# Recurrence and soft mixture of experts: output stored in units of 16 rows per partition instead of 8, with the short last part stored early

## The chip, the cores and the metric

The kernel runs on one core of one Trainium2 chip. The metric is the device time in microseconds of one execution; lower is better. Before the change the median of four runs is 205.44 us (204.38 to 205.74). The profile is one further execution, taken by the hardware profiler.

## The reference

Four sequences of 5056 tokens with 256 channels go through a gated recurrence, and its output through a soft mixture of experts with 8 experts of 4 slots, so 32 slots. Cut to what matters:

```python
sig = 1.0 / (1.0 + np.exp(-f_logit))
f = lower_bound + (1.0 - lower_bound) * sig
for t in range(S):                       # S = 5056, 4 sequences
    h = f[:, t] * h + (1.0 - f[:, t]) * x[:, t]
    y[:, t] = h
x = y.reshape(4 * 5056, 256)

logits = x @ phi                         # 20224 x 32
d = softmax(logits, axis=0)              # over all tokens
slot_input = d.T @ x                     # 32 x 256
slot_out = relu(slot_input[e] @ w1[e]) @ w2[e]    # per expert, 4 slots each
c = softmax(logits, axis=1)              # over the 32 slots
out = c @ slot_out                       # 20224 x 256, float32
```

The output is 20.7 MB. None of it can be computed before `slot_out` is known, and `slot_out` needs the logits of all tokens.

## The kernel before, in words

The first stage reads 41.4 MB of `f_logit` and `x` in 40 units of 512 tokens of one sequence. ScalarE makes the gates (L188), GpSimd the products (L199), TensorE transposes both to channels (L214), VectorE runs the scan (L247), TensorE transposes the result back to tokens (L260) and makes logits (L288), and ScalarE writes their exponentials, without the division, into `etall` as bf16: the 32 slots of the four sequences stand on 128 partitions, the tokens along the free dimension (L297). The order of this stage is written out by hand in the loop over `n`. Of the ten groups of 512 tokens the last begins at 4544, so that it ends at 5056, and the group before it, `odd`, has 448 tokens.

The weights `w1` and `w2` (16.8 MB read) are loaded by GpSimd's queue, beside the first stage and after it. The middle stage (L505 to L603) runs the experts on the 32 slots and ends in `slot_out`, which L603 scales. Inside it the row sums of `etall` over the slots are made as matmuls with ones (`row_sums`, L321), some before the experts and the others after the first eighth of the last accumulation; `rrow` gets their reciprocals (L529, L602). The 64 tokens of each sequence that don't fill three rows of 128 partitions stand in `left`, which four GpSimd copies fill (`left_over`, L331).

The store stage (L606 to L684) computes and stores the output. A matmul (L622) has 128 tokens' weights from `etall` as its stationary operand, read with a step of `n_r` tokens, and `slot_out` as its moving operand, and gives 128 tokens by 256 channels in `op` (PSUM, four buffers of four such rows). VectorE (`by_vector`, L611, four rows in one instruction) or ScalarE (`by_scalar`, L616, one row in each) multiplies by the reciprocal row sum into `ob` (SBUF), and SyncE's queue stores `ob`. With `n_r` rows per partition, partition `p` holds tokens `p * n_r` to `p * n_r + n_r - 1` of its unit, so each partition's store is one run of `n_r` KB in memory.

Before, a unit is 1024 tokens of one sequence, `n_r` = 8, 1 MB; there are 16 (L659), of which the first goes out in six pieces (L656). After them come, for each sequence, 384 tokens with `n_r` = 3 (L667), the left-over 64 tokens of all sequences in two stores (L683), and the last 512 tokens with `n_r` = 4 (L667). `ob` has four buffers; a buffer is taken again when its store has landed.

Of the kernel before, what the change touches and what calls it, by code (L numbers as in the profile page):

```python
# [9 lines left out]
F32 = mybir.dt.float32  # L10
# [8 lines left out]
def kernel(  # L19
# [40 lines left out]
    def part_rows(g):  # L60
        return R3 if g == odd else R
# [45 lines left out]
    etall = store.tile([P, n_grp * G], BF16, name="etall")  # L107
    rrow = store.tile([P, n_grp, R, B], F32, name="rrow")
# [29 lines left out]
    with tc.tile_pool(name="sp2", bufs=3) as sp2, \  # L138
# [154 lines left out]
        def exps(g):  # L293
            gs = batch_of(g)
            if g == gs[-1]:
                T = sum(rows(i) for i in gs) * R
                nc.scalar.activation(etall[:, ds(gs[0] * G, T)], lgs[0][:, :T], ACT.Exp,  # L297
                                     accum_out=csum[:, ds(g, 1)])

        def weights_to_tokens(g):  # L300
            gs = batch_of(g)
            if g != gs[-1]:
                return
            ep = plg.tile([P, 2, R, P], BF16, name="ep", tag="lg")
            for i, k in enumerate(gs):
                n_p = rows(k)
                ew = etall[:, ds(k * G, n_p * R)].rearrange("s (p r) -> s p r", r=R)
                for r in range(R):
                    nc.tensor.transpose(ep[:n_p, i, r], ew[:, :, r], ident)
            et = etok.tile([P, 2, R, B, NS], BF16, name="et", tag="et")  # L310
            n_p, k = rows(g), len(gs)
            nc.vector.tensor_copy(et[:n_p, :k].rearrange("p g r b s -> p (g r b s)"),  # L312
                                  ep[:n_p, :k].rearrange("p g r s -> p (g r s)"))
            for i, k in enumerate(gs):
                ets[k] = et[:, i]

        def row_sums(g):
            n_r = part_rows(g) if g >= odd else 2 * R
            ew = etall[:, ds(g * G, P * n_r)].rearrange("s (p r) -> s p r", r=n_r)
            for r in range(n_r):  # L320
                nc.tensor.matmul(rs_ps[:, g + r // R, r % R], ew[:, :, r], ones,  # L321
                                 start=True, stop=True, skip_group_check=True)
            if g == odd:
                nc.tensor.matmul(rs_ps[:, g, R3, ds(0, B // 2)],
                                 left.rearrange("s t u -> s (t u)"), pair_ones,
                                 start=True, stop=True, skip_group_check=True)

        def left_over():
            for b in range(B):
                k = ds(b * NS, NS)  # L330
                nc.gpsimd.tensor_copy(left[k, :, b % 2], etall[k, ds(odd * G + P * R3, L)])  # L331
# [29 lines left out]
        def late_exps(bs):  # L361
            k = ds(bs[0] * NS, len(bs) * NS)
            nc.scalar.activation(etall[k, ds(last * G, G)], lgs[0][k, ds(G, G)], ACT.Exp,
                                 accum_out=csum[k, ds(last, 1)])

        def late_weights(bs, copy):
            k, w = ds(bs[0] * NS, len(bs) * NS), len(bs) * NS
            ew = etall[k, ds(last * G, G)].rearrange("s (p r) -> s p r", r=R)
# [7 lines left out]
        def odd_weights():  # L376
            n_p = rows(odd)
            ets[odd] = etok.tile([P, R, B, NS], BF16, name="et", tag="et")
            ew = etall[:, ds(odd * G, n_p * R)].rearrange("s (p r) -> s p r", r=R)
# [30 lines left out]
        for n in range(n_unit):  # L410
# [10 lines left out]
            else:  # L421
# [34 lines left out]
                if n == n_unit - 2:  # L456
                    tail = psp.tile([P, 2, G], F32, name="tail", tag="sp")
                    rs_ps = tail[:, 0, ds(0, n_grp * R * B)].rearrange(
                        "p (g r b) -> p g r b", r=R, b=B)
# [5 lines left out]
                    left_over()  # L465
# [5 lines left out]
            if n == n_unit - 1:  # L471
                logits(last, [0, 1, 2])
                late_exps([0, 1, 2])
                for g in range(0, 4, 2):
                    row_sums(g)
# [22 lines left out]
        late_exps([3])  # L498
        to_tokens(n_unit - 1)
# [16 lines left out]
    with tc.tile_pool(name="ew", bufs=1) as ew, \  # L516
# [12 lines left out]
        nc.vector.reciprocal(rrow[:, :4], rs_ps[:, :4])  # L529
# [56 lines left out]
        for j in range(Q):  # L586
# [5 lines left out]
            if j == 0:  # L592
                nc.tensor.matmul(so_ps, rep2, so4, start=False, stop=False,
                                 skip_group_check=True)
                for g in [*range(4, odd, 2), odd, last]:
                    row_sums(g)
                for part, ps in ((rrow[:, 4:odd], rs_ps[:, 4:odd]),
                                 (rrow[:, odd, ds(0, R3)], rs_ps[:, odd, ds(0, R3)]),
                                 (rrow[:, odd, R3, ds(0, B // 2)],
                                  rs_ps[:, odd, R3, ds(0, B // 2)]),  # L600
                                 (rrow[:, last], rs_ps[:, last])):
                    nc.vector.reciprocal(part, ps)  # L602
# [4 lines left out]
    with tc.tile_pool(name="pout", bufs=4, space=PSUM) as pout, \  # L607
         tc.tile_pool(name="osb", bufs=4) as osb:

        def by_vector(ob, op, r, k, scale):  # L610
            nc.vector.tensor_tensor(ob[:, ds(r, k)], op[:, ds(r, k)],  # L611
                                    scale.broadcast_to([P, k, D]), ALU.mult)

        def by_scalar(ob, op, r0, k, scale):
            for i in range(k):
                nc.scalar.activation(ob[:, r0 + i], op[:, r0 + i], ACT.Copy, scale=scale[:, i])  # L616

        def share(g, n_r, b, rs):
            op = pout.tile([P, R, D], F32, name="op", tag="op")
            ew = etall[:, ds(g * G, P * n_r)].rearrange("s (p r) -> s p r", r=n_r)  # L620
            for i, r in enumerate(rs):
                nc.tensor.matmul(op[:, i], ew[ds(b * NS, NS), :, r],  # L622
                                 slot_out[ds(b * NS, NS), :],
                                 start=True, stop=True, skip_group_check=True)
            return op

        def rows_of(g, n_r, b):
            return out[ds(b * S + first(g), P * n_r)].rearrange("(p r) d -> p r d", r=n_r)

        for g in range(0, odd, 2):  # L630
            scales = rrow[:, ds(g, 2)].rearrange("p g r b -> p (g r) b")
            for b in range(B):
                n_r = 2 * R
                dst = rows_of(g, n_r, b)
                head = g == 0 and b == 0
                scale = scales[:, :, ds(b, 1)]
                if not head:
                    ob = osb.tile([P, n_r, D], F32, name="ob", tag="ob")
                for h in range(2):
                    ops = [share(g, n_r, b, range(h * R, h * R + R))] if not head else [  # L640
                        share(g, n_r, b, range(r, r + R // 2))
                        for r in (h * R // 2, R + h * R // 2)]
                    if not head:
                        by = by_vector if h == 0 else by_scalar
                        by(ob[:, ds(h * R, R)], ops[0], 0, R, scale[:, ds(h * R, R)])
                        continue
                    if h == 0:
                        obs = [osb.tile([P, n_r, D], F32, name="ob", tag="ob")
                               for _ in range(2)]
                    k = 1 if h == 0 else 2  # L650
                    for i in range(0, R // 2, k):
                        for j, by in enumerate((by_vector, by_scalar)):
                            r = h * R // 2 + i
                            by(obs[j][:, ds(h * R // 2, R // 2)], ops[j], i, k,
                               scale[:, ds(j * R + r, k)])
                            nc.sync.dma_start(out=dst[:, ds(j * R + r, k)],  # L656
                                              in_=obs[j][:, ds(r, k)])
                if not head:
                    nc.sync.dma_start(out=dst, in_=ob)  # L659

        for g in (odd, last):
            n_r = part_rows(g)
            for b in range(B):
                ob = osb.tile([P, R, D], F32, name="ob", tag="ob")
                by = (by_vector, by_scalar)[b % 2]
                by(ob, share(g, n_r, b, range(n_r)), 0, n_r, rrow[:, g, ds(0, n_r), ds(b, 1)])
                nc.sync.dma_start(out=rows_of(g, n_r, b), in_=ob[:, :n_r])  # L667
            if g == odd:
                n_p = B // 2
                op = pout.tile([P, R, D], F32, name="op", tag="op")  # L670
                ob = osb.tile([P, R, D], F32, name="ob", tag="ob")
                for j in range(n_p):
                    k = ds(j * 2 * NS, 2 * NS)
                    nc.tensor.matmul(op[:, j * R // n_p], left[k].rearrange("s t u -> s (t u)"),
                                     slot_out[k, :], start=True, stop=True,
                                     skip_group_check=True)
                scale = rrow[:, odd, R3, ds(0, n_p)].unsqueeze(2)
                nc.vector.tensor_tensor(
                    ob[:, ds(0, n_p)], op.rearrange("p (j k) d -> p k j d", j=n_p)[:, 0],
                    scale.broadcast_to([P, n_p, D]), ALU.mult)  # L680
                for j in range(n_p):
                    dst = out.rearrange("(b t) d -> t b d", b=B)
                    nc.sync.dma_start(  # L683
                        out=dst[ds(first(odd) + P * R3, L), ds(2 * j, 2)], in_=ob[:, j])  # L684
# [30 lines left out]
```

## Time and profile before

| What | Value |
|---|---|
| median of 4 runs | 205.44 us (204.38 to 205.74) |
| the profiled execution: time, span | 204.62 us, 202.9 us |
| busy: PE, DVE, ACT, POOL | 134.8, 144.9, 139.2, 99.2 us |
| moved by DMA | 70.74 MB, mean 349 GB/s |
| HBM read, written | 58.23 MB, 20.71 MB |
| 1 MB stores (L659) | 15, median 8.1 us from issue to landing |
| 512 KB stores (L667, last group) | 4, median 3.2 us |
| first store issued, by SyncE's queue | 148.46 us |
| end of the last store packet | 201.3 us |

The busy times are totals over stages that have different limits; which of them bounds a stage is read from the waits of that stage. A DMA's rate counts the bytes that it writes: the weights arrive as float32 and are written as bf16, so their rate of about 210 GB/s is twice that in reads. PEclk in the profile is the clock granted to TensorE, in tenths; it is 5 in the store stage from 152 us on.

### The profile page before, as it was taken

To read this page: it belongs to the slowest core of one execution; us is meant where nothing else is said; L and a number is where in the kernel's file an instruction comes from. 1 tells how busy PE (TensorE), PEld (TensorE's weight loads), DVE (VectorE), ACT (ScalarE), POOL (GpSimd) and SP (SyncE) were. 2 spreads that over 40 slices of the span, in tenths; PEclk is the share of its full clock that TensorE was granted. 3 is DMA by queue.
4 is the path that set the end of the run, shared out by engine and by line. 5 is a ranking of instruction groups with operands and counts; after the bars stand their busy time and mean duration, and the time that the engine had idled before them with its cause. 6 is when DMAs were issued, how large, how long until landed. Compare 5 with 4: busy or idle time off the path is not lost.

```text
span 202.9 us, 3118 instructions
## 1 busy us (share of the span) xinstructions
PE 134.8 (66%) x1096; PEld 100.4 (49%) x1097; DVE 144.9 (71%) x164; ACT 139.2 (69%) x195; POOL 99.2 (49%) x70
## 2 busy tenths in 40 slices
PE   0585484973966767595876776989879577762320
PEld 0364363763756546574655565657765344431110
DVE  1699869797897999979999999724184445553160
ACT  3588665899986999879988596533077666663260
POOL 2488586894978459971996959930000000000000
PEclk9999979698896999969999999999995555555555
DMA  5999999999999999999999999999449999999986
GB/s 196 412 411 409 409 413 407 407 410 308 427 405 368 358 417 408 336 395 397 373 287 406 322 237 210 216 211 216 90 168 420 417 417 423 418 423 414 407 318 266
DMA packets 19054, 70.74 MB, mean 349 GB/s; under 512 B 2256, under 2 KB 3536, under 8 KB 17120
## 3 DMA queue, kind: packets, MB, share of 16 engines
q1 hardware_dynamic: 16560, 62.14, 76.7%
q0 software_dynamic: 2336, 8.42, 20.7%
q8 instruction: 8, 0.13, 0.3%
q14 instruction: 6, 0.05, 0.1%
q10 hardware_dynamic: 144, 0.00, 0.0%
HBM read 58.23 MB, written 20.71 MB: 389 GB/s over the span
## 4 chain that ended last, share of the span: by engine, by line
DMA 44%; DVE 22%; PE 13%; ACT 8%; issue 7%; POOL 3%; SPq 0%; ACTq 0%; DVEq 0%; POOLq 0%
DMA out_dram<-ob 17%; DVE h L247 15%; DMA f_t<-in_f_logit_dram 11%; DMA w_sb<-in_moe_w_dram 9%; DMA x_t<-in_x_dram 8%; PE hp L260 3%; PE sp L214 3%; DVE ht L274 3%; DVE ob L611 3%; ACT s_t L188 2%; ACT ob L616 2%; PE up L214 2%; PE op L622 2%; ACT a L237 2%; POOL w_sb L122 2%
## 5 line engine op out<-in xcount | busy, mean ns | idle before, releaser
L199 POOL TENSOR_TENSOR u_t<-s_t,x_t 128x1024 bf16<-128x1024 bf16 (+1 forms) x39 | 82.5, 2127 | 29.4 <-ACT s_t L188 22.1
L247 DVE TENSOR_TENSOR_SCAN h<-a,h,up 128x512 bf16<-128x512 f32 (+1 forms) x72 | 86.2, 1250 | 5.3 <-PE up L214 3.7
L260 PE MATMUL hp<-ident_f,h 128*128 128x128 f32 (+1 forms) x160 | 31.6, 324 | 31.4 <-DVE ht L274 19.4
L616 ACT ACTIVATE ob<-op,rrow 128x256 f32<-128x256 f32 x78 | 30.3, 480 | 27.0 <-DMA out_dram<-ob 17.8
L188 ACT ACTIVATE s_t<-f_t 128x2048 bf16<-128x2048 f32 (+2 forms) x23 | 38.5, 1673 | 12.9 <-DMA f_t<-in_f_logit_dram 12.8
L237 ACT ACTIVATE a<-sp,nomlb 128x1024 f32<-128x1024 bf16 (+2 forms) x46 | 43.3, 992 | 5.2 <-PE sp L214 4.3
L260 PEld LDWEIGHTS hp<-ident_f,h 128*128 128x128 f32 (+1 forms) x160 | 23.2, 208 | 41.9 <-DVE ht L274 24.0
L622 PE MATMUL op<-slot_out,etall 32*128 32x256 bf16 x156 | 31.1, 382 | 15.1 <-DVE ob L611 10.2
L611 DVE TENSOR_TENSOR ob<-op,rrow 128x1024 f32<-128x1024 f32 (+3 forms) x22 | 23.9, 1101 | 22.4 <-DMA out_dram<-ob 18.2
L622 PEld LDWEIGHTS <-etall 32*128 32x128 bf16 x156 | 18.9, 147 | 26.9 <-issue 22.4
L214 PE MATMUL sp<-ident_f,s_t 128*128 128x128 f32 x144 | 23.5, 312 | 9.2 <-ACT s_t L188 5.9
L214 PE MATMUL up<-ident_f,u_t 128*128 128x128 f32 x144 | 25.3, 304 | 0.8 <-POOL u_t L199 0.8
L214 PEld LDWEIGHTS sp<-ident_f,s_t 128*128 128x128 f32 x144 | 19.6, 164 | 10.5 <-issue 5.9
L214 PEld LDWEIGHTS up<-ident_f,u_t 128*128 128x128 f32 x144 | 19.6, 160 | 1.9 <-POOL u_t L199 1.2
L274 DVE COPY ht<-hp 128x512 f32<-128x512 f32 (+1 forms) x22 | 14.7, 670 | 3.1 <-PE hp L260 3.1
L274 ACT COPY ht<-hp 128x512 f32<-128x512 f32 (+1 forms) x18 | 10.4, 580 | 5.3 <-PE hp L260 5.3
L247 DVE TENSOR_TENSOR_SCAN h<-a,up 128x512 bf16<-128x512 f32 x8 | 9.4, 1210 | 0.8 <-PE up L214 0.7
L288 PE MATMUL lg<-h,phi 128*32 128x512 bf16 (+1 forms) x80 | 7.3, 413 | 0.0
L338 PE MATMUL slot_ps<-ht,et 128*32 128x256 bf16 (+1 forms) x144 | 6.0, 289 | 0.8 <-DVE et L312 0.8
L188 ACT ACT_TABLE_LOAD x4 | 5.1, 1283 | 1.2 <-PEq L699 1.2
L297 ACT ACT_TABLE_LOAD x4 | 5.1, 1283 | 0.1
L338 PEld LDWEIGHTS <-et 128*32 128x32 bf16 (+1 forms) x144 | 3.5, 99 | 2.7 <-DVE et L312 0.9
(88 smaller groups left out, 89.1 us busy)
## 6 DMA issues: line engine op xcount, KB each, us to landing
f_t<-in_f_logit_dram SPq DMA_DIRECT2D x36, 512.0 KB, 10.7
x_t<-in_x_dram SPq DMA_DIRECT2D x36, 512.0 KB, 10.6
out_dram<-ob SPq DMA_DIRECT2D x15, 1024.0 KB, 8.1
w_sb<-in_moe_w_dram POOLq DMA_DIRECT2D x16, 512.0 KB, 8.8
out_dram<-ob SPq DMA_DIRECT2D x4, 512.0 KB, 3.2
f_t<-in_f_logit_dram SPq DMA_DIRECT2D x4, 384.0 KB, 7.7
x_t<-in_x_dram SPq DMA_DIRECT2D x4, 384.0 KB, 6.8
out_dram<-ob SPq DMA_DIRECT2D x4, 384.0 KB, 4.8
```

The source lines that it names most:

```text
L188: nc.scalar.activation(s_t, f_t, ACT.Sigmoid, scale=-1.0)
L199: nc.gpsimd.tensor_tensor(uts[n][:, :r], s_t[:, :r], x_t[:, :r], ALU.mult)
L214: nc.tensor.transpose(ps[:, :, r], t[:, r], ident_f)
L237: nc.scalar.activation(decays[n // 2, o][:, ds(n % 2, k), :T], sp[:, ds(n % 2, k), :T, o], ACT.Identity, scale=nomlb[:, ds(o, 1)], bias=1.0)
L247: nc.vector.tensor_tensor_scan(h[:, :T, o], decays[n // 2, o][:, n % 2, :T], up[:, :T, o], hs[n - B][:, ds(used(n // B - 1) - 1, 1), o] if ...
L260: nc.tensor.transpose(hp[:n_p, r], hw[:, :n_p, r], ident_f)
L274: copy(hts[g][:n_p, b].rearrange("p r d -> p (r d)").bitcast(F32), hps.pop(n)[:n_p].rearrange("p r c -> p (r c)"))
L288: nc.tensor.matmul(lg[ds(b * NS, NS), :], phi[:, o], hs[g * B + b][:, :T, o], start=o == 0, stop=o == DC - 1, skip_group_check=True)
L338: nc.tensor.matmul(slot_ps[ds(b * NS, NS), :], et[:n_p, r, b], ht[:n_p, b, r], start=(g == 0 and r == 0), stop=(g == n_grp - 1 and r == R ...
L611: nc.vector.tensor_tensor(ob[:, ds(r, k)], op[:, ds(r, k)], scale.broadcast_to([P, k, D]), ALU.mult)
L616: nc.scalar.activation(ob[:, r0 + i], op[:, r0 + i], ACT.Copy, scale=scale[:, i])
L622: nc.tensor.matmul(op[:, i], ew[ds(b * NS, NS), :, r], slot_out[ds(b * NS, NS), :], start=True, stop=True, skip_group_check=True)
```

## The change

The output is cut into `blocks`. Two blocks have 2048 tokens of each sequence with `n_r` = 16 (stores of 2 MB, 16 KB per partition); a third, `end`, has the following 896 tokens with `n_r` = 7 (896 KB, 7 KB per partition); the last 64 tokens of each sequence are the left-over ones. The order becomes: the first unit of the first block in eight pieces of 1, 1, 2, 2, 3, 3, 2 and 2 rows (`pieces`); the four 7-row units (`whole(end, b)`); the left-over tokens in two stores (`rest`); and then the other seven 16-row units (`whole`). In a 16-row unit VectorE scales the first and third four rows and ScalarE the second and fourth; in a 7-row unit VectorE scales four rows and ScalarE three. `ob` has six buffers, of 16 KB per partition.

`etall` now has no gap: groups stand at their first token, not at a multiple of 512. `row_sums` goes by block, 16 matmuls ahead of the experts and 16 + 7 + 1 later, as many as before, and two of the four later reciprocals go. Since the left-over tokens are now the last 64 of a sequence, `left_over` comes after the last exponentials, behind GpSimd's two memsets instead of ahead of them.

```diff
-    etall = store.tile([P, n_grp * G], BF16, name="etall")
-    rrow = store.tile([P, n_grp, R, B], F32, name="rrow")
+    wide_r = 4 * R
+    n_blk = (S // (P * wide_r))
+    blocks = [(i * P * wide_r, wide_r) for i in range(n_blk)]
+    blocks.append((n_blk * P * wide_r, (S - n_blk * P * wide_r) // P))
+    etall = store.tile([P, S], BF16, name="etall")
+    rrow = store.tile([P, n_grp * R, B], F32, name="rrow")
...
-        def row_sums(g):
-            n_r = part_rows(g) if g >= odd else 2 * R
-            ew = etall[:, ds(g * G, P * n_r)].rearrange("s (p r) -> s p r", r=n_r)
+        def row_sums(i):
+            t0, n_r = blocks[i]
+            ew = etall[:, ds(t0, P * n_r)].rearrange("s (p r) -> s p r", r=n_r)
...
                     exps(odd)
-                    left_over()
...
-                for g in range(0, 4, 2):
-                    row_sums(g)
+                row_sums(0)
...
         late_exps([3])
+        left_over()
...
-                for g in [*range(4, odd, 2), odd, last]:
-                    row_sums(g)
...
-                    nc.vector.reciprocal(part, ps)
+                for i in range(1, len(blocks)):
+                    row_sums(i)
+                q = n_grp * R - 1
+                nc.vector.reciprocal(rrow[:, wide_r:q], rs_ps[:, wide_r:q])
+                nc.vector.reciprocal(rrow[:, q, ds(0, B // 2)], rs_ps[:, q, ds(0, B // 2)])
...
-         tc.tile_pool(name="osb", bufs=4) as osb:
+         tc.tile_pool(name="osb", bufs=6) as osb:
...
+        def pieces(i, b, sizes):
+            dst = rows_of(i, b)
+            obs = [osb.tile([P, blocks[i][1], D], F32, name="ob", tag="ob") for _ in range(2)]
+            r = 0
+            for pair in sizes:
+                ops = [pout.tile([P, R, D], F32, name="op", tag="op") for _ in range(2)]
+                at = [0, 0]
+                for k in pair:
+                    todo = []
+                    for j in range(2):
+                        share(ops[j][:, ds(at[j], k)], i, b, r, k)
+                        todo.append((r, at[j]))
+                        r, at[j] = r + k, at[j] + k
+                    for j, by in enumerate((by_vector, by_scalar)):
+                        q, o = todo[j]
+                        by(obs[j][:, ds(q, k)], ops[j][:, ds(o, k)], scale_of(i, b, q, k))
+                        nc.sync.dma_start(out=dst[:, ds(q, k)], in_=obs[j][:, ds(q, k)])
+
+        def whole(i, b):
+            n_r = blocks[i][1]
+            ob = osb.tile([P, n_r, D], F32, name="ob", tag="ob")
+            for j, r in enumerate(range(0, n_r, R)):
+                k = min(R, n_r - r)
+                op = pout.tile([P, R, D], F32, name="op", tag="op")
+                share(op, i, b, r, k)
+                by = (by_vector, by_scalar)[j % 2]
+                by(ob[:, ds(r, k)], op[:, ds(0, k)], scale_of(i, b, r, k))
+            nc.sync.dma_start(out=rows_of(i, b), in_=ob)
...
+        end = len(blocks) - 1
+        pieces(0, 0, [(1, 2), (3,), (2,)])
+        for b in range(B):
+            whole(end, b)
+        rest()
+        for i in range(end):
+            for b in range(B):
+                if i or b:
+                    whole(i, b)
```

`share`, `rows_of`, `by_vector` and `by_scalar` do what they did, by block; `rest` is the left-over code as it was, with `ob` of two rows.

## The prediction

> **What bounds the kernel now.** I read the slices of the span first, then the chain that ended last, then the waits, and last the store stage in windows. The slices show DMA at nine tenths nearly throughout:
>
> ```profile
> DMA  5999999999999999999999999999449999999986
> GB/s 196 412 411 409 409 413 407 407 410 308 427 405 368 358 417 408 336 395 397 373 287 406 322 237 210 216 211 216 90 168 420 417 417 423 418 423 414 407 318 266
> ```
>
> The reader is to see two holes: slices 29 and 30 (about 143 to 152 us), between the last load and the full store stream, and the last two slices (193 us on). The chain of waits, by engine and line, agrees:
>
> ```profile
> DMA 44%; DVE 22%; PE 13%; ACT 8%; issue 7%; POOL 3%; SPq 0%; ACTq 0%; DVEq 0%; POOLq 0%
> DMA out_dram<-ob 17%; DVE h L247 15%; DMA f_t<-in_f_logit_dram 11%; DMA w_sb<-in_moe_w_dram 9%; DMA x_t<-in_x_dram 8%; PE hp L260 3%; PE sp L214 3%; DVE ht L274 3%; DVE ob L611 3%; ACT s_t L188 2%; ACT ob L616 2%; PE up L214 2%; PE op L622 2%; ACT a L237 2%; POOL w_sb L122 2%
> ```
>
> Waits after 145 us (who waits, for whom: us in total, times, longest):
>
> ```profile
> DVE ob L611 <- DMA out_dram<-ob: 18.2, 13, 4.0
> ACT ob L616 <- DMA out_dram<-ob: 17.8, 13, 3.7
> ...
> PE so_ps L588 <- DMA w_sb<-in_moe_w_dram: 0.7, 1, 0.7
> ```
>
> DVE and ACT wait for stores to free `ob`, so transfers bound the store stage; and just before it PE waits 0.7 us for the last weight load, so transfers also set when that stage begins. The stage in windows (us from the start: length, busy time of PE, PEld, DVE, ACT, POOL, granted clock, DMA share, GB/s):
>
> ```profile
> 149.00:150.00 1.00, 1.00 (x14) 0.99 (x14) 0.85 (x2) 0.89 (x4) 0.00 (x0) 1.00 0.55 187
> 150.00:151.00 1.00, 0.70 (x7) 0.46 (x5) 1.00 (x2) 1.00 (x4) 0.00 (x0) 1.00 0.80 269
> 151.00:152.00 1.00, 0.81 (x8) 0.64 (x8) 0.76 (x1) 1.00 (x5) 0.00 (x0) 0.63 0.92 336
> ...
> 158.00:183.00 25.00, 17.86 (x78) 10.47 (x78) 12.86 (x11) 16.29 (x43) 0.00 (x0) 0.50 1.01 420
> 183.00:193.00 10.00, 3.53 (x16) 1.63 (x16) 2.37 (x4) 2.95 (x8) 0.00 (x0) 0.50 1.01 412
> 193.00:194.00 1.00, 0.89 (x7) 0.65 (x7) 0.68 (x2) 0.06 (x1) 0.00 (x0) 0.50 0.30 117
> 194.00:195.00 1.00, 0.58 (x4) 0.10 (x1) 1.00 (x1) 0.30 (x1) 0.00 (x0) 0.50 0.98 383
> 195.00:196.00 1.00, 0.00 (x0) 0.00 (x0) 0.41 (x2) 1.00 (x4) 0.00 (x0) 0.50 0.79 269
> 196.00:201.00 5.00, 0.00 (x0) 0.00 (x0) 0.88 (x1) 1.84 (x5) 0.00 (x0) 0.50 1.01 406
> 201.00:202.90 1.90, 0.00 (x0) 0.00 (x0) 0.00 (x0) 0.00 (x0) 0.00 (x0) 0.50 0.07 24
> ```
>
> The stream is full from 152 to 193; from 193 to 196 the missing shares are 0.70 + 0.02 + 0.21 = 0.93 us. So what can be won lies in the ramp, the tail and the cost of a byte. No compute engine is full from 158 to 183.
>
> **What the Trainium skill says.** (1) "DMA: Bandwidth & Descriptors", section "Why small descriptors are slow": each packet carries a fixed overhead. The trace agrees: store packets of 1, 2, 3, 4 and 8 KB have medians of 46, 84, 121, 159 and 313 ns, that is about 8 ns plus 38.1 ns per KB. (2) Same page, "Anatomy of one DMA": about 2 us per transfer does not scale with size, most of it the completion. The smallest store here lands 2.1 us after issue. (3) "Advanced Engine Details and Errata", section "SBUF Cachelines": lines of 16 bytes, of which two accesses each are needed for full speed. The row sums (L321, full clock) show it: weight reads with a token step of 3, 4 and 8 bf16 follow one another after 26, 33 and 60 ns. (4) "TensorE: Matmul & The Clock Gate", "Back-to-back issue gap": 256 columns at the low clock take N/1.2 = 213 ns; the trace has L622 matmuls exactly 213 ns apart from 152 us on.
>
> **The change part by part.** The profiled execution took 204.62 us with a span of 202.9, 0.8 under the median of 205.44; I work out a difference in the span and take it from the median.
>
> *Before the stores: 0.* Loads and scans stay. `left_over` (4 POOL copies, 1.14 us) moves behind POOL's two memsets (0.95 and 3.51 us); all `w_sb` loads are issued on POOL by 128 us, so no DMA is moved past. It now waits for the last exponentials, which end at 132.6; its reader runs at 143. Row sums stay 16 + 24 matmuls with steps 16 and 7 for 8, 3 and 4: step 7 costs at most 4 x 34 + 3 x 27 = 0.2 us; step 16 costs nothing if every read already touches its own line, and up to another 60 ns each (1.9 us for 32) if it costs double. I take 0 for that. Two of four reciprocals go (about 0.3 us of 0.82). The cover of all this is PE's 0.7 us wait for weights; without that cover the worst case is 1.9 + 0.2 - 0.7 = 1.4 us.
>
> *The ramp: -0.1 (from -0.5 to +0.3).* Before, DVE starts after two matmuls of one tile (147.90), ACT after four (148.17). Now each waits for one row: about 147.80 and 147.92. In the compiled order the next rows of the same two PSUM tiles wait for DVE's and ACT's first row (0.42, 0.47 us): two matmuls plus 0.27 us latency later DVE has two rows at 148.7, 0.1 later than now. SP takes about 0.45 us per piece, and the first packet starts 0.85 us after the first issue (148.46, 149.31). Eight pieces then issue at about 148.35, 148.75, 149.45, 149.95, 150.45, 151.0, 151.5, 152.0. At 0.38, 0.69 and 0.97 us of engine time for one, two and three rows, the stream starts at 149.2, misses 0.35 us near 150, and ends the pieces at 155.0, as if it had been full from 149.6; before, the same sum gives 149.7. The first 7-row store (4 rows on DVE 1.22, 3 on ACT 1.2) issues at 153.2, in time; the first 16-row one near 161.6 with queued work until 164.5, also in time.
>
> *The packets: -0.4 (from -0.65 to +0.5).* Engine time over the stage, 8 packets per store and engine. Before: pieces 4 x 8 x 46 + 2 x 8 x 84 = 2.8; fifteen units 15 x 8 x 313 = 37.6; 3-row 4 x 8 x 121 = 3.9; 1 KB 16 x 46 = 0.7; 4-row 4 x 8 x 159 = 5.1; with completions (9 ns per store) 50.35 us. After: pieces 8 x (92 + 4 x 84 + 242) = 5.4; 7 KB 32 x 275 = 8.8; 0.7; seven units 56 x 618 to 626 = 34.6 to 35.1; with completions 49.7 to 50.2. The 16 KB packet is not in the trace's stores: twice the 8 KB packet and the line above bound it, and I take the middle; nothing shown excludes that a long packet holds the writes up, so I keep 2% on it (+0.7) as the bad end.
>
> *The tail: -0.6 (0 to -1.2).* Now the last stores are small and four `ob` buffers hold few bytes, so the queue runs dry. Afterwards seven 2 MB stores end it; a unit needs 16 x 0.213 = 3.4 us of PE, 2 x 1.22 of DVE and 8 x 0.39 = 3.1 of ACT against 5.0 of DMA, so the backlog grows and six buffers suffice; the last store is issued near 184. Not all of the 0.93 us comes back. At 152.94 an instruction fetch (a 16 KB packet, 1.28 us) holds one DMA engine: the sixteen landing events of the first whole unit then lie 2.0 us apart, those of the fifteenth 1.2, those of the last store 0.2. The late engine ends the kernel, and in the holes it still had work; its own idle time there is about 0.25 us. With no hole to catch up in, it should end about 0.9 us after the others. Followed alone: pieces landed at 157.2, 7-row stores +8.6, rest +0.7, seven units at twice its 2.44 us, less 4 x 9 ns, +34.0, so 200.5 against 201.69 now: -1.2. The three terms add up to -1.1; I take **-1.2 us**.
>
> **Rivals.** (A) As above: 205.44 - 1.2 = 204.2. (B) The late engine catches up or no fetch falls there: then only the sum counts, 149.6 + 49.7 + 0.4 (the last packet's landing) = 199.7 against 201.69, -2.0: 203.4. For it: its lag shrinks 0.06 us per MB; against: it took fifteen units to lose 0.8. (C) The engines stay apart and the 16 KB packet gains nothing (or is cut in two inside): -0.5, 204.9. For it: 8 KB packets already move 420 GB/s. (D) Slower: weight reads with a step of 16 make PE the bound. A read takes 162 ns at the low clock, hidden under 213; if a row came to take p, PE would work on the seven units (112 rows) from 156.4 (28 rows at 213 ns after 150.4) + 1.4 us on, and the end would be 157.8 + 112p + 1.6 (ACT) + 0.95 (issue, first byte) + 5.0 (the last 2 MB, now uncovered) + 1.55. It passes 203.9, half a percent late, from p = 0.33 us; at 0.34 it gives +2.1, 207.5. Against it: a doubled read is 324 ns, just short, and the step of 8 already takes a line per element. It speaks for it that no step of 16 is in the trace.
>
> **How the numbers follow.** Half a percent (1.03 us) is about what a measurement of this kernel tells from no change. A 0.40, B 0.28, C 0.21, D 0.11. A lies just beyond the half percent: 0.27 faster, 0.13 same. B is all faster; C 0.02 faster, 0.19 same; D slower. Sum 0.57, 0.32, 0.11. The range from 203.0 to 205.4 takes A to C with the bounds above and leaves out D.
>
> **What would show it.** Right: DMA share near 1.0 from 152 to the end, no hole after 193, the last store issued near 184, waits of DVE and ACT for `ob` nearly gone, 16 KB packets near 620 ns, PE rows still 213 ns apart. Wrong: rows over 213 ns apart or PE waiting on nothing while DMA starves; a hole near 161 before the first 16-row store; row sums that push the last `so_ps` matmuls past 145.9; 16 KB packets over 640 ns, which would cost 0.8 us and more.

## The result, and the profile after

The changed kernel takes 204.11 us (median of 44 runs, 203.01 to 205.81) against 205.07 (63 runs, 203.92 to 206.64) for the kernel before: a ratio of 0.9956 with an interval of 0.9941 to 0.9971. That is 0.9 us or 0.44% less. The interval leaves out 1, so the gain is real, but it is a quarter smaller than the -1.2 us that was forecast. The profiled spans are 201.9 and 202.9 us.

The slices of the changed kernel's page:

```profile
DMA  6999999999999999999999999999539999999993
GB/s 187 413 409 409 412 408 407 409 409 312 418 407 388 338 414 406 326 406 396 389 329 398 315 230 213 213 215 213 116 134 393 423 414 445 425 415 415 448 435 162
```

Slices 31 to 39 are all at nine tenths: the hole after 193 us is gone. The ramp (slices 29 and 30) is still there. The chain of the same page:

```profile
DMA 35%; PE 20%; DVE 18%; ACT 9%; issue 5%; SPq 1%; ACTq 0%; DVEq 0%
```

DMA has less of the chain than before (35% against 44%), so compute seems to have become the bound. The waits after 145 us say what happened (who waits, for whom: us in total, times, longest):

```profile
ACT ob L614 <- PE op L620: 7.0, 2, 6.6
DVE ob L610 <- PE op L620: 5.8, 9, 1.7
...
ACT ob L614 <- DMA out_dram<-ob: 1.5, 1, 1.5
```

DVE and ACT waited 36.0 us for `ob` before; 1.5 is left. With six buffers of 2 MB they run ahead of the stores, so the chain goes back through them although the stores still end last: the wait that ends the kernel is now SyncE's, at the end of its queue.

```profile
SPq L707 <- DMA out_dram<-ob: 21.2, 2, 16.4
```

The windows of the store stage (length, busy time of PE, PEld, DVE, ACT, POOL, granted clock, DMA share, GB/s):

```profile
149.00:150.00 1.00, 1.00 (x9) 0.80 (x7) 1.00 (x2) 1.00 (x4) 0.00 (x0) 1.00 0.77 248
150.00:151.00 1.00, 0.87 (x9) 0.63 (x9) 0.92 (x3) 1.00 (x5) 0.00 (x0) 1.00 0.70 252
151.00:152.00 1.00, 0.93 (x10) 0.61 (x8) 1.00 (x2) 1.00 (x4) 0.00 (x0) 0.81 1.03 384
...
158.00:183.00 25.00, 18.24 (x100) 12.90 (x99) 16.42 (x14) 20.42 (x56) 0.00 (x0) 0.50 1.01 423
183.00:193.00 10.00, 0.00 (x0) 0.00 (x0) 0.00 (x0) 0.00 (x0) 0.00 (x0) 0.50 1.01 428
193.00:196.00 3.00, 0.00 (x0) 0.00 (x0) 0.00 (x0) 0.00 (x0) 0.00 (x0) 0.50 0.96 410
...
199.00:201.00 2.00, 0.00 (x0) 0.00 (x0) 0.00 (x0) 0.00 (x0) 0.00 (x0) 0.50 0.04 16
```

From 183 on no compute engine works, and the share stays near 1. Look at the last line: with 4% busy for two microseconds, the end is neither a full stream nor an empty one. It is one DMA engine of sixteen, finishing alone. A share is a mean over sixteen engines and hides that; the landing events of each store, sixteen of them, show it. For the last store fifteen come between 199.43 and 199.68, and the sixteenth at 200.65. From here on that engine is the late engine (times in us; spread is the last event minus the first):

| Store | before: last landing, spread | after: last landing, spread |
|---|---|---|
| the one that completes the first 2 MB | 157.55, 2.00 | 157.46, 1.96 |
| before: the 14th 1 MB unit after it; after: the fourth 7-row unit | 191.75, 1.23 | 165.97, 1.68 |
| last store of all | 201.69, 0.22 | 200.65, 1.22 |

Followed along the last landings, the difference can be read term by term (us). The rows say where the time went, not yet what caused it:

| Part | before | after | difference |
|---|---|---|---|
| start of `slot_out` | 146.96 | 146.88 | -0.08 |
| from there to the landing of the first 2 MB | 10.59 | 10.58 | -0.01 |
| the other 14 MB (14 units of 1 MB, or seven of 2 MB) | 34.20 | 34.00 | -0.20 |
| 3-row and 4-row stores, or 7-row stores | 9.10 | 8.51 | -0.59 |
| left-over tokens | 0.84 | 0.68 | -0.16 |
| sum: last landing | 201.69 | 200.65 | -1.04 |

### The profile page after: what moved, and what is told of

The parts are those of the page before. It is cut to its first block, busy times and chain, and to the rows that moved or that the text cites. A ratio compares the mean times of both kernels' runs of the same rounds, so it can differ in the third digit from the quotient of the medians.

```text
span 201.9 us, 3055 instructions
## 1 busy us (share of the span) xinstructions
PE 131.2 (65%) x1096; PEld 101.1 (50%) x1097; DVE 144.6 (72%) x162; ACT 137.2 (68%) x193; POOL 99.2 (49%) x70
## 4 chain that ended last, share of the span: by engine, by line
DMA 35%; PE 20%; DVE 18%; ACT 9%; issue 5%; SPq 1%; ACTq 0%; DVEq 0%
DMA f_t<-in_f_logit_dram 28%; DVE h L250 13%; ACT ob L614 7%; DMA x_t<-in_x_dram 4%; PE op L620 4%; PE hp L263 3%; DVE ht L277 3%; DMA out_dram<-ob 3%; PE so_ps L590 2%; PE sp L217 2%; PE up L217 2%; DVE ob L610 1%; PE slot_ps L341 1%; SPq L181 1%; PE tail L324 1%
## 5 line engine op out<-in xcount | busy, mean ns | idle before, releaser
L614 ACT ACTIVATE ob<-op,rrow 128x256 f32<-128x256 f32 x76 | 28.4, 500 | 9.1 <-PE op L620 7.0
L620 PE MATMUL op<-slot_out,etall 32*128 32x256 bf16 x156 | 27.9, 386 | 2.3 <-ACT ob L614 0.9
L610 DVE TENSOR_TENSOR ob<-op,rrow 128x1024 f32<-128x1024 f32 (+3 forms) x23 | 24.4, 1104 | 5.9 <-PE op L620 5.8
L620 PEld LDWEIGHTS <-etall 32*128 32x128 bf16 x156 | 19.8, 152 | 9.9 <-issue 5.3
```

The source lines that it names most:

```text
L610: nc.vector.tensor_tensor(ob, op, scale.broadcast_to(list(ob.shape)), ALU.mult)
L614: nc.scalar.activation(ob[:, i], op[:, i], ACT.Copy, scale=scale[:, i])
L620: nc.tensor.matmul(op[:, j], ew[:, :, r + j], slot_out[ds(b * NS, NS), :], start=True, stop=True, skip_group_check=True)
```

## The experiments

Ratios are against the kernel before, with their intervals; each experiment had its own runs of it (medians from 204.92 to 205.06), so a ratio isn't the quotient of two medians in this text. "Stage" is the time from the first store packet to the last landing: 52.38 us before, 51.53 after. "Spread" is that of the sixteen landings of one store. Stage and spread come from one profiled execution of each kernel. Some of these lie 1 to 2 us from the kernel's median, largely because their stores begin earlier or later, so times from the start of the span are not compared between kernels.

### Was it the hole after 193 us? (x_tail, x_bufs)

The prediction put the largest term, -0.6, on the hole, and gave the small last stores and the four buffers as its cause. The first kernel is before with only the order changed, the second before with only the buffers changed.

```diff
+        units(True)          # x_tail: the first unit
+        short_ones()         # 3-row, left-over, 4-row
+        units(False)         # the other fifteen units
```
```diff
-         tc.tile_pool(name="osb", bufs=4) as osb:
+         tc.tile_pool(name="osb", bufs=8) as osb:   # x_bufs
```

> The kernel before with its order alone changed: after the first unit come the 3-row stores, the left-over tokens and the 4-row stores, then the other fifteen 8-row units; four ob buffers and all sizes as before. Late-engine theory (the end is set by the one DMA engine that an instruction fetch held for 1.3 us near 153 us; the tail's hole was idle time of the others): only that engine's own idle comes back, 0.2 to 0.35 us, so 204.8 against 205.07, and the sixteen landings of the last store lie 0.9 to 1.2 us apart instead of 0.2. Hole theory (the whole missing share after 193 us counts): 0.9 us less, 204.2, landings of the last store within 0.3 us.

> The kernel before with eight ob buffers instead of four, order and sizes as before. Late-engine theory: the hole after 193 us closes (DMA share 0.95 and more from 193 to 196), the last store's landings lie about 1.1 us apart, and the gain is again 0.2 to 0.35 us. If it was the order and not the buffers: the hole stays and the time is that of before. Hole theory: 0.9 us less.

x_tail: 205.34 us, ratio 1.0016 (0.9988 to 1.0044), stage 52.62. Its windows:

```profile
160.00:161.00 1.00, 0.97 (x4) 0.62 (x4) 0.38 (x1) 1.00 (x4) 0.00 (x0) 0.50 0.45 180
...
193.00:196.00 3.00, 0.00 (x0) 0.00 (x0) 0.00 (x0) 0.24 (x1) 0.00 (x0) 0.50 1.01 421
```

The hole is gone from 193 and stands at 160 instead, after the short stores. There is no gain. The expected spread of the last store (0.9 to 1.2) was wrong, it is 0.3: the late engine caught up in the new hole, where its spread falls from 1.51 to 0.49.

x_bufs: 204.66 us, ratio 0.9985 (0.9964 to 1.0006), stage 52.70. Its windows:

```profile
183.00:193.00 10.00, 2.01 (x8) 0.80 (x7) 2.27 (x3) 2.58 (x7) 0.00 (x0) 0.50 1.01 412
193.00:196.00 3.00, 0.00 (x0) 0.00 (x0) 0.86 (x1) 1.57 (x4) 0.00 (x0) 0.50 1.03 385
```

Here the hole is closed altogether, and the spread of the last store is 1.13 in place of 0.22. A gain of 0.9 us (0.9956) lies outside the interval. The 0.2 to 0.35 us that the late-engine theory expected lies inside, and so does no gain at all. The stage is not shorter, but in this execution the late engine fell 2.44 us behind, against 2.00 before. So a full stream to the end gives little: most of what was idle in the hole was not the engine that ends the kernel.

### What makes the one engine late? (x_nofetch, z_nofetch, z_fetch)

The suspect is an instruction fetch: a 16 KB packet that the profile lists under the kind `instruction`, on queue q8. In the first two kernels nearly all matmuls of the store stage are left out, so that TensorE runs fewer instructions; the stores are the same. In the third, 50 small matmuls are added among the scans, to move TensorE's last fetch out of the store stage.

```diff
+        def row_of(g, n_r, b, h):                  # x_nofetch, on before
+            if not same:
+                same.extend(share(g, n_r, b, range(1)) for _ in range(2))
+            return same[h][:, ds(0, 1)].broadcast_to([P, 2 * R, D])
```
```diff
-                share(op, i, b, r, k)              # z_nofetch, on after, in `whole`
+                op = same[j % 2]                   # two matmuls' rows serve all units
...
-                by(ob[:, ds(r, k)], op[:, ds(0, k)], scale_of(i, b, r, k))
+                by(ob[:, ds(r, k)], op[:, ds(0, 1)].broadcast_to([P, k, D]), ...)
```
```diff
+                if 14 <= n < 34:                   # z_fetch, on after
+                    pad(2 + n % 2)                 # so many matmuls of 32 columns
```

> The kernel before with all but ten of the store stage's matmuls left out (the units after the pieces scale the rows of two matmuls, so their output values are not the reference's; DVE, ACT and every store do the same work), so that no instruction fetch falls into its store stage. Late-engine theory: a buffer of ob waits for the landing on all sixteen engines, so the hole after 193 us was itself a trace of the late engine; without the fetch landings lie within 0.3 us, most of the hole goes although order and buffers stay, and the time is about 1.0 us under before: 204.1. The change is then worth the same 0.9 us without a fetch (z_nofetch had 203.2). If the hole came from four buffers with few bytes: the hole stays, 0.5 us or less gained.

> The changed kernel with 138 of the store stage's 158 matmuls left out: the eleven units after the pieces all scale the rows of two matmuls, so their output values are not the reference's; DVE, ACT and every store do the same work. TensorE's instruction stream then ends before its last fetch. Late-engine theory: no 16 KB instruction packet after 144 us, the sixteen landings of the last store within 0.3 us (1.2 in the changed kernel), the end about 1.0 us sooner, so 203.1 against 204.1 and some 1.9 us under the kernel before. If the lag of the last engine costs nothing, or comes from somewhere else: the time of the changed kernel, within 0.3 us.

> The changed kernel with 50 small matmuls more (32 columns, into a part of PSUM that nobody reads), two or three in each of twenty steps of the first stage, where PE idles half the time: they move TensorE's instruction fetches 100 instructions earlier, the last one from 155 us to about 147 us, where no store runs. Late-engine theory: the landings of the last store come together (from 1.2 us apart to 0.3 or less) and the end comes about 0.9 us sooner than in the changed kernel, 1.8 us under the kernel before. If the last engine lags for another reason: landings still 1.2 us apart, time of the changed kernel or, if the matmuls get in the way of the first stage, later.

x_nofetch: 203.97 us, ratio 0.9956 (0.9931 to 0.9981), stage 51.79, as expected; spread 0.2 to 0.3 from the first 1 MB unit on. Its windows, with order and buffers as before:

```profile
193.00:194.00 1.00, 0.00 (x0) 0.00 (x0) 0.57 (x1) 0.63 (x2) 0.00 (x0) 0.50 1.03 402
194.00:195.00 1.00, 0.00 (x0) 0.00 (x0) 0.77 (x2) 0.00 (x0) 0.00 (x0) 0.50 1.04 402
195.00:196.00 1.00, 0.00 (x0) 0.00 (x0) 0.58 (x1) 0.63 (x2) 0.00 (x0) 0.50 0.97 372
```

The hole is gone with neither its stores nor its buffers touched. An `ob` buffer comes free when all sixteen landings are there, so fifteen engines wait, through `ob`, for one. The matmuls that are missing here don't explain it: in before, ScalarE and VectorE begin their rows 0.10 to 0.19 us after the landing that frees their buffer (191.75 and 191.86, 192.71 and 192.83, 193.65 and 193.84, 194.60 and 194.70), and here 0.07 to 0.12 us after it.

z_nofetch: 203.21 us, ratio 0.9922 (0.9895 to 0.9950), stage 50.58; spread 0.2. This is as expected. In the DMA view from 149 us on, the changed kernel has one 16 KB packet on queue q8 (queue: packets, MB, share of 16 engines):

```profile
q1 hardware_dynamic: 3024, 20.71, 91.0%
q8 instruction: 1, 0.02, 0.1%
```

z_nofetch has none there. Its matmuls are also gone, so it alone does not tell the packet from TensorE's work; z_fetch does. That the packets of q8 are TensorE's shows in their places: in every run that has an eighth one, it starts when 1963 to 1998 TensorE instructions have been recorded (its sequencer's own counted too), and x_nofetch and z_nofetch have 1934 and 1950 in all.

z_fetch: 204.68 us, ratio 0.9974 (0.9955 to 0.9993), stage 52.03. The eighth fetch moved to 145.1 us, as meant, but a ninth came, at 172.14, which was not foreseen. Until then the spread is 0.15 to 0.21 at every 7- and 16-row store. The same DMA view, from 168 to 176 us:

```profile
q1 hardware_dynamic: 235, 3.34, 99.6%
q8 instruction: 1, 0.02, 0.7%
```

The next landing, at 175.55 to 177.58, has a spread of 2.03, and the last store one of 1.72. The lag appears where the packet is, and the matmuls that ran from 158 to 171 made none. So the fetch makes the engine late, and the miss of this experiment is its best evidence. The packets themselves show how. While the fetch runs, from 172.14 to 173.07, fifteen store packets are under way and not sixteen, so it has taken the place of one. Followed by starts and ends that meet, the two store packets ahead of it take 833 and 978 ns and the one behind it 1005, in place of 615: with the 931 ns of the fetch that is 1.90 us lost on one engine, and the spread has grown by 1.82. The last landing lags more here than in after (1.72 against 1.22), since fewer stores are left to catch up in; that this costs time shows in the stage (52.03 against 51.53), while the ratios overlap.

### What are the larger packets worth? (y_8k, y_8k_nofetch, x_seven)

y_8k is after with 1024-token units (8 KB packets) and 12 buffers of half the size; y_8k_nofetch is y_8k with the edit of z_nofetch. x_seven has the order, the 1 MB units and the four buffers of before, with 7-row units in place of the 3-row and 4-row ones; it is built from after, so the left-over tokens come last and the row sums go by block.

```diff
-    wide_r = 4 * R
+    wide_r = 2 * R                                # y_8k, y_8k_nofetch
...
-         tc.tile_pool(name="osb", bufs=6) as osb:
+         tc.tile_pool(name="osb", bufs=12) as osb:
...
-        pieces(0, 0, [(1, 2), (3,), (2,)])
+        pieces(0, 0, [(1, 2), (1,)])
```

> The changed kernel with 8 rows per unit instead of 16 (8 KB runs; first unit in six pieces of 1, 1, 2, 2, 1, 1 rows; twelve ob buffers of half the size; the row sums of two blocks ahead of the experts, so that their number there stays). Packet theory: 8 KB packets take 313 ns and 16 KB packets 615, so 56 x 11 ns = 0.6 us of engine time comes back, and it is 0.3 us under the kernel before instead of 0.9. If the length of the runs buys nothing: the time of the changed kernel, within 0.2 us.

> The changed kernel with 8-row units (as y_8k) and with the same matmuls left out as in z_nofetch. Packet theory: with no late engine the mean engine time decides, 50.5 us against 49.9, so the store stage from the first packet to the last landing takes 51.2 us against 50.6 in z_nofetch, and the time is 203.8 against 203.2. If packets of 16 KB buy nothing even then: 50.6 and 203.2.

> The kernel before with one part of the change: the last 960 tokens of each sequence in 7-row stores and the left-over tokens at the end, in place of 3-row, left-over and 4-row stores; 8-row units, four ob buffers, six pieces as before, order as before. Late-engine theory: followed along the last engine's landings, the 3-row and 4-row stores took 9.1 us before and the 7-row stores 8.5 in the changed kernel, so 0.4 to 0.6 us of the gain comes back here: 204.5. If buffers, order or ramp brought the gain: within 0.2 us of before.

| Kernel | us | ratio | stage | time of data packets, mean of 16 engines |
|---|---|---|---|---|
| before | 205.07 | 1 | 52.38 | 50.65 |
| after | 204.11 | 0.9956 (0.9941 to 0.9971) | 51.53 | 49.88 |
| y_8k | 204.17 | 0.9946 (0.9925 to 0.9967) | 51.81 | 50.50 |
| z_nofetch | 203.21 | 0.9922 (0.9895 to 0.9950) | 50.58 | 49.87 |
| y_8k_nofetch | 202.71 (6 runs) | 0.9889 (0.9842 to 0.9936) | 51.13 | 50.50 |
| x_seven | 204.61 | 0.9998 (0.9973 to 1.0024) | 52.79 | 50.43 |

On the mean engine 16 KB packets save 0.62 us (50.50 to 49.88). On the stage they save 0.28 with the fetch and 0.55 without it, in one execution each. The late engine would explain the gap: a punctual engine takes 2.50 us for a 1 MB unit and 4.91 for a 2 MB one, the late engine 2.443 and 4.86, so that it saves only 0.03 per 2 MB. The times show none of it. y_8k was expected only 0.3 us under before and is as fast as after, and y_8k_nofetch, expected at 203.8, lies even below z_nofetch, with overlapping intervals. So the times don't bear out what was expected of the packets; what 16 KB packets save is seen in the traces only.

x_seven's 7-row stores and left-over ones take 9.29 us along the last landings, against 9.94 before, -0.65. Its ratio shows no gain; in its profiled execution the late engine fell 2.65 us behind in place of 2.0. One more thing is to be seen there. It has four buffers, the order of before, a late engine (spread 1.70 to 1.85 at the 7-row stores), and yet no hole:

```profile
193.00:196.00 3.00, 0.00 (x0) 0.00 (x0) 1.33 (x2) 1.21 (x3) 0.00 (x0) 0.50 1.02 421
```

So the hole of before needed three things together: the late engine (x_nofetch), few buffers (x_bufs) and small last stores (x_seven). Take one away, and it is gone.

### Order and ramp (y_last, y_ramp)

```diff
-        pieces(0, 0, [(1, 2), (3,), (2,)])
+        pieces(0, 0, [(4,), (4,)])                 # y_ramp: four pieces in place of eight
```

y_last is after with the 7-row units and `rest` moved to the end, behind the 16-row ones.

> The changed kernel with the order of before: the 7-row units and the left-over tokens last. Late-engine theory: six buffers keep the queue full, so the order costs nothing: 204.1, the time of the changed kernel within 0.3 us, no hole at the end. If the order brought the gain: 0.5 us or more back towards 205.07, with a hole after 193 us.

> The changed kernel with the first unit in four pieces of four rows instead of eight of 1, 1, 2, 2, 3, 3, 2, 2. The first piece then needs four matmuls and one DVE instruction of 1.22 us, so the first packet comes about 1.2 us later; the stream misses nothing after it, so as if full from 150.4 instead of 149.6. Late-engine theory: a late start holds up every engine, the late one too, so 0.6 to 0.8 us over the changed kernel: 204.8. If the pieces buy nothing: 204.1.

y_last: 204.46 us, ratio 0.9963 (0.9941 to 0.9985); stage 51.66. The order costs nothing that is seen. (In its profiled execution, of 206.38 us, `slot_out` started 2.5 us later than in after's, so only the stage is compared.) No hole was expected, but there is one, between the pieces and the first 16-row store:

```profile
157.00:160.00 3.00, 2.62 (x17) 1.93 (x16) 2.69 (x3) 3.00 (x10) 0.00 (x0) 0.50 0.62 250
```

The late engine catches up in it (spread from 1.97 to 0.69, at the end 0.27). As in x_tail, a hole of about 1.1 us in the mean share hardly lengthens the stage, because the late engine has work in it.

y_ramp: 203.87 us, ratio 0.9953 (0.9931 to 0.9975). The first packet starts at 150.27, 1.15 us later than in after, but the last landing comes only 0.38 us later after the start of `slot_out` (54.15 against 53.77), less than expected. Four pieces have longer packets (49.53 us of engine time against 49.88), which the expectation left out. The rest is the ramp of after, where the share is only 0.77 and 0.70 from 149 to 151, while y_ramp's stream is full from its first packet on. The eight small pieces are not what made the kernel faster.

### A version with the fetch ahead of the stores (v_pair)

Here the second block and the 7-row units are computed for two sequences in one matmul of 512 columns, with `slot_two` holding the two sequences' `slot_out` block-diagonally: 112 store matmuls in place of 158. 45 small matmuls among the scans put the eighth fetch into the pause between loads and stores.

```diff
+        for b in range(B):
+            k = ds(b * NS, NS)
+            nc.gpsimd.tensor_copy(slot_two[k, b % 2], slot_out[k])
...
+                    nc.tensor.matmul(op[:, ds(2 * j, 2)].rearrange("p b d -> p (b d)"),
+                                     ew[:, :, r + j],
+                                     slot_two[rows2].rearrange("s b d -> s (b d)"),
+                                     start=True, stop=True, skip_group_check=True)
...
+                if 14 <= n < 34:
+                    pad(2 + (n % 4 == 0))
```

> A version meant to keep the gain that the late engine takes: the changed kernel with the 7-row units and the second block computed for two sequences in one matmul of 512 columns (slot_out spread over a block-diagonal copy, made by POOL), so the store stage has 112 matmuls and not 158, and 45 small matmuls more in the first stage, which move TensorE's last instruction fetch to about 146 us, where no store runs and no weight load does. Late-engine theory: no 16 KB instruction packet between 148 us and the end, landings of the last store within 0.3 us, 203.1 to 203.3 us. If the fetch lands on the last weight load instead: 0.5 us later than that. If the lag does not decide: 204.1.

203.12 us (6 runs), ratio 0.9911 (0.9881 to 0.9942), stage 50.50. The eighth fetch is at 145.25; the DMA view from 149 us on has the same stores and no packet of q8 (the one left, of 8 KB on q14, is at 149.52, ahead of the first store packet):

```profile
q1 hardware_dynamic: 3024, 20.71, 91.0%
q14 instruction: 1, 0.01, 0.1%
```

From the third piece on the spread stays at 0.2 to 0.3, and the stage is as short as z_nofetch's, which leaves the matmuls out. It is 0.9% faster than before; its interval ends where after's begins. The place of the fetch follows from a count of instructions, so every edit of this kernel moves it.

## Why the prediction was right or wrong

**Size and mechanism.** The forecast followed the late engine by hand, and this was right nearly term by term: pieces landed 157.2 (157.46 measured), 7-row stores 8.6 (8.51), rest 0.7 (0.68), seven units 34.0 (34.00), last landing 200.5 (200.65). The forecast of -1.2 stands against -1.04 in the profiled executions and -0.9 by the ratio, within the range and somewhat too large. The other way to the number, the sum of three terms (-1.1), came close in part by luck, as the terms show.

**Before the stores: 0.** Right (-0.08). Row sums with a step of 16 follow one another after 61.5 ns, against 60 for the step of 8: the step of 8 had the full cost already. (The step of 7 takes 53.5 ns. The prediction swapped two counts in its bound for it: three rows had a step of 3 and four a step of 4. It stays 0.2 us.) The last `so_ps` matmuls start at 145.81, before at 145.89. The cover was thinner than the 0.7 us that one execution showed: PE's wait for the last weights is 0.06 us in after's.

**The ramp: -0.1.** It gave 0.0, inside the bounds. The first packet starts 0.2 us earlier, but the hole at 150 that was foreseen is there (share 0.70): the third piece was issued at 149.33, when VectorE had just scaled its two rows (149.30). SyncE needed 853 and 1025 ns for the last two issues, not 450, but these began at 151.40 and 152.29, when the stream was full. (The 2 us of fixed time that the prediction quotes under (2) is stated there for transfers issued by GpSimd; the smallest stores of SyncE's queue take 2.1 us before and 2.2 after.)

**The packets: -0.4.** Mis-sized, and for the wrong engine. The 16 KB packet takes 615 ns (618 to 626 was assumed), and mean engine time falls by 0.77 us; but on the late engine the big units give only 0.20. The sum over engine time is the right one only for a kernel in which all engines end together.

**The tail: -0.6.** The size came out (-0.59 - 0.16 along the last landings), the reason only in part: of the prediction's steps this one failed. "Now the last stores are small and four `ob` buffers hold few bytes, so the queue runs dry" leaves out the late engine, without which there is no hole (x_nofetch), and closing the hole is not what a gain of 0.6 us comes from: the ratio of x_bufs is 0.9985 with an interval that takes in 1, and x_seven, whose stream has no hole, gains nothing that its times show. Nor is all of -0.75 due to larger packets. By the medians, packets and completions of these stores take 9.79 us of engine time before and 9.62 after, which is 0.17. Before needed 0.15 us more than that sum, and after 0.43 less, since its late engine was catching up there (spread from 1.96 to 1.63).

**The rivals.** A is what happened. B, "no fetch falls there", was put at 203.4; with the fetch kept out of the stores, z_nofetch and v_pair are at 203.2 and 203.1. D is refuted: rows are still 213 ns apart, and the last store is issued at 178.9, sooner than the 184 of the prediction. Of C, the premise that 16 KB packets gain nothing is not refuted by the times (y_8k), but 204.9 is 0.8 us too slow.

**What stays open.** Which part of the change brings the 0.9 us is not shown by times. Without the new order (y_last), the small pieces (y_ramp) or the 16 KB packets (y_8k) the gain is still there; larger last stores alone (x_seven) and more buffers alone (x_bufs) bring none that is clear of noise, and the two together without the rest were not run. Why the store packets next to a fetch take longer is open too, and why the late engine then moves the same bytes 1 to 2% faster than the others. The traces don't name a packet's engine; that the late engine is the one with the fetch rests on the timing above. Without a fetch on either side the change would be worth 1.2 us of stage (51.79 to 50.58) and 0.0034 of ratio, by x_nofetch and z_nofetch, whose intervals overlap.

## What to carry to other kernels

A mean DMA share near 1 doesn't say that the stage is as short as its bytes: compare the first and the last of the sixteen landings of a store, and if they are a microsecond or more apart, find the engine and what it carried. A hole in the mean share can be the others waiting for that engine through the buffers; closing it with more buffers or another order then gained little or nothing here. In a stage that only moves data, the place of an instruction fetch can be worth more than the size of the packets: fewer TensorE instructions in the stage and some more ahead of it gave 0.45% here (v_pair against after, where the intervals just touch), the 16 KB packets nothing that the times show.

## What of the hardware was not expected

- TensorE's instruction fetch is a 16 KB packet on one of the DMA engines that carry the stores: 8 packets for the 2193 recorded matmuls and weight loads of after. Among stores it takes 0.93 to 1.78 us, and the spread of the landings goes from 0.2 to between 2.0 and 2.65 us, in part because neighbouring store packets take longer too (833, 978 and 1005 ns in place of 615 in z_fetch). In a full stream the engine makes up only 0.05 to 0.07 us per store.
- The 8 KB packets of queue q14 leave a smaller mark of the same kind: in before one falls among the pieces (149.76), and their spread goes up to 0.85 us; in y_ramp both such packets come ahead of the first store packet, and the first two pieces have a spread of 0.12 and 0.15.
- Store packets take 48, 86, 124.5, 275 and 615 ns for 1, 2, 3, 7 and 16 KB (after): still about 8 ns and 38 ns per KB, with no penalty for the long ones.
